# Narrower PE tiles for the state's read, float32r for its gates from part three, and one PE step for two products with the state

## The chip, the cores and the metric

The kernel runs on one core of a Trainium2 chip. Its time is the device time of one execution in microseconds; before the change the median of three runs is 759.64 us (759.14 to 759.84). The core has engines that run side by side and wait for each other through semaphores: TensorE (PE in the profile, with its weight loads as PEld) multiplies matrices from SBUF into PSUM, VectorE (DVE) and ScalarE (ACT) work element by element and move PSUM to SBUF, GpSimd (POOL) helps DVE with a few elementwise steps, and SyncE (SP) issues the DMAs. PSUM has 8 banks here, each 512 float32 columns wide (tile `PS`). A stationary operand that fills only a part of the 128x128 array leaves room for others beside it; `tile_position=(row, column)` says where it goes, and a piece of the array used so is called a tile of PE below.

## What is computed

Three layers follow each other. Attention with a small state (4 batches, 8 heads, 512 tokens, 32 state rows of 64 numbers a head), then a gated layer, then a softplus layer:

```python
scores = scale * np.matmul(x, state.transpose(0, 1, 3, 2))
...
xread = np.matmul(a, state)
scores2 = scale * np.matmul(state, x.transpose(0, 1, 3, 2))
...
sread = np.matmul(a2, x)
...
a = x @ w_a
b = x @ w_b
return (a * b @ w_out).astype(np.float32)
...
h = x @ w_in
g = np.maximum(h, 0.0) + np.log1p(np.exp(-np.abs(h)))
return (g @ w_out).astype(np.float32)
```

`a` and `a2` are softmaxes of the scores. A batch has 512 tokens from `xread` and 32 from `sread`, so there are 2176 tokens. The gated layer has 1536 hidden columns and the softplus layer 2048. All weights arrive in float64; the kernel reads their halves as integers and builds float32 from them.

## The kernel before

A planner at build time holds all the work as steps in program order. A step is one DVE or ACT instruction, or a group of matmuls on PE (class `Products`, closed by `end`, L493). The planner walks a clock with costs of its own; on each engine it takes, among the steps whose inputs it thinks ready, the one that stands first in program order and whose buffers it can place. An engine's queue is then fixed, and at run time each engine works through its queue in order. Nearly all instructions come from helpers: matmuls from L476, transposes from L491, copies and casts from L422 (ACT) or L423 (DVE), two-input DVE and POOL work from L430.

The gated layer runs in six parts of 256 hidden columns (`s` = 0 to 5; "part three" is `s` = 2), each over four batches `b`:

- `state_softmax(b)`, L726: transposes the scores with 8 PE transposes, makes the softmax over 32 state rows with six DVE instructions and an exponential on ACT, and transposes the result back with 8 more (`turned(e)`, L741). The last DVE instruction before these is the multiply with the reciprocal sum, L740.
- `state_w(s, bp, g)`, L765: the products of the state with the weights of part `s`, for two batches and four heads: 8 float32 matmuls with 64 rows and 32 columns each, in the eight 64x32 tiles of PE, into two banks. A cast and a subtract (`split_to`, L500) then make a high and a low float32r piece. A float32 matmul is two records in the profile, a float32r matmul one.
- `gates_of(s, b)`, L823, takes a batch's softmax times these products, 24 float32r matmuls of 512 columns (three for each float32 product, `three` at L479); `y_part`, L849, takes the gates times `w_out`, 24 more.
- `sread(b)`, L677, is the state's read of the tokens, in part 0 only: 16 float32 matmuls of 128 rows, 64 columns and 128 moving columns (two heads at once, L698), whose diagonal 64x64 blocks are what is wanted; then two scalings on ACT, two transposes and four copies into `srT`.
- `read_x(s)`, L792, gives the gates of the 128 state tokens: four float32 matmuls of 512 columns from `srt` and the weights `ab`, and `read_y` (L866) goes on with them. Parts 0 and 1 of it run in part 1, the others each in their own part.
- `bring`, `bring_wo`, `bring_w2` convert weights (L524: one ACT and five DVE or POOL instructions for 1024 columns).

The softplus layer (L979 on) follows with a loop over 4 quarters of the hidden columns, 4 batches and 4 steps.

Of the kernel before, what the change touches and what calls it, by code (L numbers as in the profile page):

```python
# [12 lines left out]
AF = mybir.ActivationFunctionType  # L13
# [4 lines left out]
P = 128  # L18
# [310 lines left out]
def attention_moe_moe2(ctx, tc, x, state, w_a, w_b, w_out, w_in, w_out2, out):  # L329
# [12 lines left out]
    B, H, S, D = x.shape  # L342
# [5 lines left out]
    KD = DM // P  # L348
# [4 lines left out]
    scale = 1.0 / float(D) ** 0.5  # L353
# [58 lines left out]
    def activation(o, i, func, **kw):  # L412
        also = [v for v in kw.values() if isinstance(v, Ref)]
        acc = [kw["accum_out"]] if "accum_out" in kw else []
        give = lambda: nc.scalar.activation(  # L415
            made(o), made(i), func, **{k: made(v) for k, v in kw.items()})
        plan.add({"act": (act_us(cols(o), in_psum(i)), give)}, [i, *also], [o, *acc])
# [82 lines left out]
    def split_to(i, hi, lo):  # L500
        copy(hi, i)
        tt(lo, i, hi.bitcast(F32), ALU.subtract)
# [102 lines left out]
    def xn(b, p, c):  # L605

        return xs[b][p].rearrange("q (h c d) -> q c h d", h=2, d=D)[:, c]
# [10 lines left out]
    for n, i in enumerate((zs, zt)):  # L618
        ps = Buf(K, 1)
# [14 lines left out]
    def quarter(b, i):  # L634

        return i ^ b % 2
# [40 lines left out]
    def sread(b):  # L677
        t = raw.pop(b)
        nm, sum2 = small(), small()
        nm_, sum_ = nm[0][:, 0:2], sum2[0][:, 0:2]  # L680
        reduce(nm_, t.all(), ALU.max)
        ts(nm_, nm_, -scale, ALU.mult)
        for g in range(2):
            activation(
                t[g], t[g], AF.Exp, bias=nm[0][:, g:g + 1], scale=scale,
                accum_out=sum2[0][:, g:g + 1],
            )
        ts(sum_, sum_, 1e-9, ALU.add)
        reciprocal(sum_)
        pa = turned(t)  # L690
        a2 = Buf(F, 2)
        copy(a2.all(), pa.all())
        pr = Buf(K, 2)
        m = Products()
        for g in range(2):
            for c in range(4):
                for j in range(2):
                    m.one(  # L698
                        pr[g][64 * j:64 * j + 64, 0:P].rearrange("p (h d) -> p h d", h=2),
                        a2[g][:, c * P + 64 * j:c * P + 64 * j + 64],  # L700
                        xn(b, 2 * g + j, c), c == 0, c == 3, us=0.23,
                    )
        m.end()

        for g in range(2):
            sd = a2[g][:, 0:P]
            activation(sd, pr[g][:, 0:P], AF.Identity, scale=sum2[0][:, g:g + 1])
            m = Products()
            m.turn(pr[g][:, P:2 * P], sd)
            m.end()  # L710
        for i in range(2):
            for g in range(2):
                src = pr[g][64 * i:64 * i + 64, P:2 * P]
                src = src.rearrange("p (j q n) -> p j q n", j=2, q=2)
                if b % 2:
                    src = src[:, :, ::-1]
                copy(
                    srT[64 * i:64 * i + 64, 2 * g:2 * g + 2, NS * b:NS * b + NS], src[:, :, i]
                )
# [42 lines left out]

        ab[s, p] = ab[s, p + 1] = fetch(("ab", s, p), 4)

    def state_w(s, bp, g):  # L765

        banks = Buf(K, 2)
        m = Products()
        for i in range(4):
            pp, half = divmod(i, 2)  # L770
            rows = slice(64 * half, 64 * half + 64)
            for j in range(2):
                b = 2 * bp + j
                q = quarter(b, i)
                m.one(
                    banks[j][32 * q:32 * q + 32], srow(sts[0], 2 * g + pp, half, NS * b, NS),
                    ab[s, 2 * g + pp][pp][rows, :], True, True, us=0.11,
                    tile_position=(64 * half, 32 * q),
                )
        m.end()  # L780
        if s == 0 and 2 * bp in G32:
            v = Buf(F, 2)
            copy(v.all(), banks.all())
            for j in range(2):
                sw[s, 2 * bp + j, g] = (v[j],)
            return
        h, l = Buf(R, 2, 8), Buf(R, 2, 6)
        split_to(banks.all(), h.all(), l.all())
        for j in range(2):
            sw[s, 2 * bp + j, g] = h[j], l[j]  # L790

    def read_x(s):  # L792

        ps = Buf(K, 1)
        m = Products()
        for p in range(KD):
            m.one(ps[0], srt[0][:, p * P:p * P + P], ab[s, p][p % 2], p == 0, p == KD - 1, us=0.87)
        m.end()
        t = Buf(F, 1)
        ab_ = t[0][:, 0:HW]  # L800
        copy(ab_, ps[0][:, 0:HW])
        tt(ab_, ab_, ps[0][:, HW:W], ALU.mult)
        pt = Buf(K, 1)
        m = Products()
        for j in range(2):
            m.turn(pt[0][:, j * P:j * P + P], t[0][:, j * P:j * P + P])
        m.end()
        if s == 0 and len(Y32) == B:
            gs[s] = Buf(F, 1)
            copy(gs[s][0][:, 0:HW], pt[0][:, 0:HW])  # L810
            return
        gs[s] = Buf(R, 1)
        split_to(pt[0][:, 0:HW], gs[s][0][:, 0:HW], gs[s][0][:, HW:W])

    gs, wo, y = {}, {}, {}

    def bring_wo(s):
        w = fetch(("wo", s), 2)
# [95 lines left out]
    scores_of(0)  # L914
    bring(0, 0)
    state_softmax(0)
    state_w(0, 0, 0)
    bring(0, 2)
    state_w(0, 0, 1)
    steps = [(s, b) for s in range(NHS) for b in range(B)]  # L920
    SREAD = 0
    pend = []
# [7 lines left out]
    for s, b in steps:  # L930
        if s == 0 and b == 0:
            scores_of(1)
        hl = gates_of(s, b)
        if s == 0:
            if b == 0:
                bring_wo(0)
                state_softmax(1)
                scores_of(2)
                state_w(0, 1, 0)
                state_w(0, 1, 1)  # L940
            if b == 1:
                state_softmax(2)
                scores_of(3)
            if b == 2:
                state_softmax(3)
        if s == SREAD:
            sread(b)
        if s and b == 0:
            if s > SREAD + 1:
                read_x(s)  # L950
            bring_wo(s)
        if s == SREAD + 1 and b < SREAD + 2:
            read_x(b)
        if s == SREAD + 1 and b == 3:
            for t in range(SREAD + 1):
                read_y(t)
        if s > SREAD and b == 2:
            read_y(s)
        if s + 1 < NHS:
            if b == 0:  # L960
                bring(s + 1, 0)
            if b == 1:
                bring(s + 1, 2)
                state_w(s + 1, 0, 0)
            if b == 2:
                state_w(s + 1, 0, 1)
                state_w(s + 1, 1, 0)
            if b == 3:
                state_w(s + 1, 1, 1)
        elif b:  # L970
            bring_w2(("in", 0) if b == 1 else ("out", 0) if b == 2 else ("in", 1))
        pend.append((s, b, hl))
        if len(pend) > 1:
            finish()
# [122 lines left out]
```

## Time and profile before

| | us |
|---|---|
| three runs, median | 759.64 |
| the profiled execution | 758.87 |
| its span, first to last instruction | 757.1 |
| PE busy / DVE busy / ACT busy in it | 733.0 / 583.4 / 401.8 |
| first matmul begins / last one ends | 7.78 / 749.97 |

The span is read from the left: until 7.78 us PE has no input; then the softmaxes and the first part set a time in which PE has waits; from 86 us on PE hardly stops until 749.97 us; a tail of 7.1 us brings the last results out. PE's granted clock is at its full level (2.4 GHz) except in the tail. Busy time counts records that overlap once.

### The profile page before, as it was taken

How to read it: one execution, taken by the hardware profiler on the slowest of the kernel's cores; microseconds unless marked ns; L12 is line 12 of the kernel's file. 1: busy time of each engine (PE TensorE's matmuls, PEld its weight loads, DVE VectorE, ACT ScalarE, POOL GpSimd, SP SyncE). 2: the span in 40 equal slices, each digit the busy share in tenths (PEclk: the TensorE clock that was granted, in tenths of full speed). 3: DMA queues.
4: the chain of work that ended last, by engine and by line, in shares of the span. 5: the costliest groups of instructions: out<-in, count | busy, mean ns of one | idle time of the engine just before them, and what ended most of it. 6: DMA issues, size and time to landing. Idle time of an engine off the chain costs nothing.

```text
span 757.1 us, 9417 instructions
## 1 busy us (share of the span) xinstructions
PE 733.0 (97%) x3828; PEld 581.8 (77%) x3828; DVE 583.4 (77%) x735; ACT 401.8 (53%) x644; POOL 32.7 (4%) x19
## 2 busy tenths in 40 slices
PE   5889999999999999999999999999999999999996
PEld 4447677777777777778888798888988889888895
DVE  4999987768677868889999767665769888665673
ACT  4767753232323424424395586656666667656562
POOL 0000000000001000000211100100110011100000
PEclk9999999999999999999999999999999999999999
DMA  9611321103112113133111000000111100001112
GB/s 309 205 59 54 130 93 54 58 1 112 56 44 68 56 56 111 56 110 114 56 56 56 1 1 1 0 1 1 55 57 56 55 1 1 1 0 56 56 56 70
DMA packets 22351, 45.17 MB, mean 60 GB/s; under 512 B 2212, under 2 KB 6308, under 8 KB 22308
## 3 DMA queue, kind: packets, MB, share of 16 engines
q1 hardware_dynamic: 21764, 43.52, 17.0%
q10 hardware_dynamic: 544, 1.05, 0.4%
q8 instruction: 30, 0.49, 0.3%
q14 instruction: 13, 0.11, 0.0%
HBM read 40.11 MB, written 4.46 MB: 59 GB/s over the span
## 4 chain that ended last, share of the span: by engine, by line
PE 77%; DVE 19%; issue 1%; DMA 1%; ACT 1%; SPq 0%; DVEq 0%
PE PS L476 76%; DVE SF L442 6%; DVE SF L430 5%; DVE SR L430 3%; DVE SM L448 2%; DVE SF L438 2%; PE PS L491 1%; DMA x<-in_x 1%; DVE xr L430 1%; ACT SF L415 0%; SPq L459 0%; DVE SM L453 0%; ACT SR L422 0%; DVE SR L423 0%; DVE xf L430 0%
## 5 line engine op out<-in xcount | busy, mean ns | idle before, releaser
L476 PE MATMUL PS<-SR 128*128 128x512 f32 (+2 forms) x1878 | 461.0, 378 | 2.5 <-DVE SF L430 1.2
L476 PEld LDWEIGHTS PS<-SR 128*128 128x128 f32 x1878 | 340.1, 188 | 71.2 <-issue 3.6
L415 ACT ACTIVATE SF<-SF 128x512 f32<-128x512 f32 (+3 forms) x259 | 165.7, 650 | 14.1 <-DMA SF<-in_moe_w_b 7.2
L476 PE MATMUL PS<-SR,xr 128*128 128x512 f32 (+2 forms) x568 | 159.3, 384 | 0.0
L430 DVE TENSOR_TENSOR SF<-SF,PS 128x1024 f32<-128x1024 f32 (+2 forms) x100 | 97.7, 985 | 47.9 <-PE PS L476 47.4
L422 ACT CAST SR<-SF 128x1024 fp32r<-128x1024 f32 (+3 forms) x103 | 75.5, 735 | 107.5 <-DVE SF L430 107.2
L442 DVE SCALAR_TENSOR_TENSOR SF<-SF 128x512 f32<-128x512 f32 (+4 forms) x139 | 131.6, 949 | 1.1
L476 PEld LDWEIGHTS PS<-SR,xr 128*128 128x128 f32 x568 | 105.0, 188 | 24.3 <-issue 2.6
L422 ACT COPY SF<-PS 128x1024 f32<-128x1024 f32 (+3 forms) x87 | 62.3, 737 | 110.2 <-PE PS L476 103.9
L476 PE MATMUL PS<-xr,SR 128*128 128x512 f32 x378 | 120.3, 392 | 0.0
L430 DVE TENSOR_TENSOR SR<-SF,SR 128x512 fp32r<-128x512 f32 (+3 forms) x96 | 82.9, 868 | 23.4 <-ACT SR L422 23.3
L442 DVE SCALAR_TENSOR_TENSOR SF<-PS,SF 128x512 f32<-128x512 f32 (+2 forms) x77 | 46.6, 605 | 54.9 <-ACT SF L415 54.9
L476 PEld LDWEIGHTS PS<-xr,SR 128*128 128x128 f32 x378 | 70.9, 188 | 16.8 <-DVE SF L430 0.8
L430 DVE TENSOR_TENSOR SF<-SF 128x512 f32<-128x512 f32 (+3 forms) x97 | 79.7, 822 | 1.7
L476 PE MATMUL PS<-SF 64*32 64x512 f32 (+2 forms) x592 | 65.2, 551 | 1.0 <-ACT SF L422 1.0
L438 DVE TENSOR_SCALAR SF<-SF 128x1024 uint32<-128x1024 uint32 x67 | 45.9, 689 | 18.8 <-ACT SF L415 18.4
L415 ACT ACTIVATE SF<-PS 128x512 f32<-128x512 f32 (+2 forms) x76 | 39.9, 526 | 30.8 <-PE PS L476 29.8
L430 POOL TENSOR_TENSOR SF<-SF 128x1024 f32<-128x1024 f32 x9 | 24.0, 2663 | 507.4 <-DVE SF L442 386.1
L476 PEld LDWEIGHTS PS<-SF 64*32 64x32 f32 (+1 forms) x592 | 22.0, 117 | 26.8 <-issue 22.6
L422 ACT CAST xr<-SF 128x1024 fp32r<-128x1024 f32 (+3 forms) x26 | 21.3, 821 | 33.9 <-DVE SF L430 33.9
L422 ACT CAST SR<-PS 128x1024 fp32r<-128x1024 f32 (+2 forms) x24 | 20.6, 866 | 20.1 <-PE PS L491 12.1
L476 PE MATMUL PS<-xr,xr 128*128 128x512 f32 x80 | 29.0, 391 | 0.0
(56 smaller groups left out, 274.1 us busy)
## 6 DMA issues: line engine op xcount, KB each, us to landing
SF<-in_moe_w_out SPq DMA_DIRECT2D x14, 1024.0 KB, 4.9
SF<-in_moe_w_in SPq DMA_DIRECT2D x8, 1024.0 KB, 5.4
SF<-in_moe_w_a SPq DMA_DIRECT2D x11, 512.0 KB, 4.1
SF<-in_moe_w_b SPq DMA_DIRECT2D x11, 512.0 KB, 5.0
x<-in_x SPq DMA_DIRECT2D x8, 512.0 KB, 9.9
out<-SF SPq DMA_DIRECT2D x13, 256.0 KB, 2.6
out<-xf SPq DMA_DIRECT2D x4, 256.0 KB, 2.6
SF<-in_moe_w_a ACTq DMA_DIRECT2D x1, 512.0 KB, 4.2
```

Of the source, the lines that this page charges most:

```text
L415: give = lambda: nc.scalar.activation(made(o), made(i), func, **{k: made(v) for k, v in kw.items()})
L422: "act": (act_us(n, ps), lambda: nc.scalar.copy(made(o), made(i))),
L430: put = lambda eng: lambda: eng.tensor_tensor(out=made(o), in0=made(a), in1=made(b), op=op)
L438: give = lambda: nc.vector.tensor_scalar(made(o), made(i), s1, None, op0=op0)
L442: give = lambda: nc.vector.scalar_tensor_tensor(out=made(o), in0=made(a), scalar=s, in1=made(b), op0=op0, op1=op1)
L448: give = lambda: nc.vector.tensor_reduce(out=made(o), in_=made(i), axis=AX.X, op=op)
L476: self.all.append(lambda: nc.tensor.matmul(made(o), made(w), made(x), start=first, stop=last, **kw))
L491: self.all.append(lambda: nc.tensor.transpose(made(o), made(i), ident))
```

## The change

`sread` takes one head a matmul: 32 matmuls a batch of 128 rows, 32 columns and 64 moving columns, head `i` at the columns `q` of PE in which its scores stand, four tiles side by side. What was a 128x128 result in one bank is 128x64, the scalings handle 64 columns, and the transposes give 64 rows instead of 128.

`state_w` is one step for both `g`: 16 matmuls into four banks, then two casts and two subtracts as before. At the start (`s` = 0, first two batches) it stays one `g` at a time. The two steps of parts 1 to 5 are put into the program at `b` = 2 and `b` = 3, where three places held four steps.

`read_x` splits `srt` once (512 columns) and the weights of a part (two splits of 1024 columns each) into float32r pieces from `s` = 2 on, and makes 12 float32r matmuls in place of four float32 ones. For `s` = 0 and 1 nothing changes in it.

```diff
-                for j in range(2):
+                for i in range(4):
+                    q = 32 * quarter(b, i)
                     m.one(
-                        pr[g][64 * j:64 * j + 64, 0:P].rearrange("p (h d) -> p h d", h=2),
-                        a2[g][:, c * P + 64 * j:c * P + 64 * j + 64],
-                        xn(b, 2 * g + j, c), c == 0, c == 3, us=0.23,
+                        pr[g][q:q + 32, 0:D], a2[g][:, c * P + q:c * P + q + 32],
+                        xn(b, 2 * g + i // 2, c)[:, i % 2], c == 0, c == 3, us=0.03,
+                        tile_position=(0, q),
                     )
...
-            sd = a2[g][:, 0:P]
-            activation(sd, pr[g][:, 0:P], AF.Identity, scale=sum2[0][:, g:g + 1])
+            sd = a2[g][:, 0:D]
+            activation(sd, pr[g][:, 0:D], AF.Identity, scale=sum2[0][:, g:g + 1])
             m = Products()
-            m.turn(pr[g][:, P:2 * P], sd)
+            m.turn(pr[g][0:D, P:2 * P], sd)
...
-    def state_w(s, bp, g):
-
-        banks = Buf(K, 2)
+    def state_w(s, bp, gs_=(0, 1)):
+
+        banks = {g: Buf(K, 2) for g in gs_}
         m = Products()
+        for g in gs_:
+            state_products(m, banks[g], s, bp, g)
+        m.end()
+        for g in gs_:
...
+            h, l = Buf(R, 2, 8), Buf(R, 2, 6)
+            split_to(banks[g].all(), h.all(), l.all())
...
+        whole = s < WHOLE
+        if not whole:
+            if not srparts:
+                srparts.append(split(srt))
+            whl = split(ab[s, 0], 6) + split(ab[s, 2], 6)
         m = Products()
         for p in range(KD):
-            m.one(ps[0], srt[0][:, p * P:p * P + P], ab[s, p][p % 2], p == 0, p == KD - 1, us=0.87)
+            c = slice(p * P, p * P + P)
+            w = [ab[s, p]] if whole else whl[p // 2 * 2:p // 2 * 2 + 2]
+            m.three(ps[0], [i[0][:, c] for i in ([srt] if whole else srparts[0])],
+                    [i[p % 2] for i in w], p == 0, p == KD - 1)
...
-                state_w(0, 1, 0)
-                state_w(0, 1, 1)
+                state_w(0, 1)
...
-                state_w(s + 1, 0, 0)
             if b == 2:
-                state_w(s + 1, 0, 1)
-                state_w(s + 1, 1, 0)
+                state_w(s + 1, 0)
             if b == 3:
-                state_w(s + 1, 1, 1)
+                state_w(s + 1, 1)
```

`state_products` holds the eight matmuls that stood in `state_w`, unchanged.

Since the planner orders all steps anew, queues change beyond the edited lines. DVE at the start, before the change; the third row is the cast of `state_w(0, 1, 0)`, the fourth its subtract, and then a weight conversion (`bring(0, 2)`) and the softmaxes' first reductions begin:

```order
L442 SCALAR_TENSOR_TENSOR SF<-SF 128x1024
L430 TENSOR_TENSOR SF<-SF 128x1024
L423 CAST SR<-PS 128x1024
L430 TENSOR_TENSOR SR<-PS,SR 128x1024
L438 TENSOR_SCALAR SF<-SF 128x1024
L448 TENSOR_REDUCE SM<-SF 128x2
L448 TENSOR_REDUCE SM<-PS 128x32
```

The same place of DVE's queue after the change:

```order
L442 SCALAR_TENSOR_TENSOR SF<-SF 128x1024
L430 TENSOR_TENSOR SF<-SF 128x1024
L438 TENSOR_SCALAR SF<-SF 128x1024
L448 TENSOR_REDUCE SM<-SF 128x2
L442 SCALAR_TENSOR_TENSOR SF<-SF 128x1024
L448 TENSOR_REDUCE SM<-PS 128x32
```

The cast has gone to ACT, the subtract stands some two dozen rows later beside that of the other `g`, and DVE's first work after its pause is now the conversion of `bring(0, 2)`. Up to the multiply of `state_softmax(2)` there are 52 DVE instructions both before and after the change; the sets differ by the cast, which left, and one subtract of `gates_of(0, 1)`, which came ahead of it.

PE in part 0, from the gates of batch 1 on, before the change. `x_82` marks `sread(0)`; the row of 32x512 is `state_w(1, 0, 0)`; the row with 6 is the first of four pieces of `y_part(0, 0)`; the last row begins with the 8 transposes of `turned(e)` of `state_softmax(2)`:

```order
L476 MATMUL PS<-x_82,SF 64x128 x16
L476 MATMUL PS<-SF 128x512 x2
L491 MATMUL PS<-ident,SF 128x128 x2
L476 MATMUL PS<-SF 32x256 x16
L476 MATMUL PS<-SF 32x512 x8
L476 MATMUL PS<-SR 128x512 x6
L491 MATMUL PS<-ident,SF 128x128 x16
```

And after the change:

```order
L476 MATMUL PS<-x_82,SF 32x64 x32
L476 MATMUL PS<-SF 128x512 x2
L491 MATMUL PS<-ident,SF 64x128 x2
L491 MATMUL PS<-ident,x_98 128x128 x8
L476 MATMUL PS<-SF 32x256 x8
L476 MATMUL PS<-SR 128x512 x6
L476 MATMUL PS<-SF 32x256 x8
L476 MATMUL PS<-SR 128x512 x12
L491 MATMUL PS<-ident,SF 128x128 x16
```

Three pieces of `y_part(0, 0)` now stand ahead of these transposes where one stood, `state_w(1, 0)` has moved behind them, and the second transposes of batch 3's tokens (`x_98`), which stood ahead of `sread(0)`, come here.

## Rows read from the trace of the kernel before

**Rows 1.** Busy time by stretch: stretch, length, then each engine's busy us (instructions).

```profile
20.00:86.00 66.00, 57.63 (x464) 36.82 (x465) 65.66 (x81) 47.49 (x72) 0.00 (x0) 1.00 0.30 101
86.00:330.00 244.00, 244.00 (x1257) 180.67 (x1257) 186.55 (x181) 89.21 (x104) 2.39 (x1) 1.00 0.20 68
330.00:400.00 70.00, 70.00 (x312) 57.76 (x311) 66.17 (x69) 38.02 (x53) 8.07 (x3) 1.00 0.25 83
400.00:750.00 350.00, 349.60 (x1672) 297.79 (x1670) 255.57 (x397) 216.66 (x404) 20.95 (x8) 1.00 0.07 25
```

**Rows 2.** Chain that ended last, to 110 us: start, us, what.

```profile
16.35 1.24 DVE SR L423
17.61 1.22 DVE SR L430
...
57.35 1.22 DVE SF L430
...
84.49 1.24 DVE SF L430
...
85.86 1.28 PE PS L491 x10
```

**Rows 3.** The same chain, its last piece.

```profile
747.29 3.41 DVE SF L430 x5
```

**Rows 4.** PE in order of time, to 100 us: start, us, what, count, idle before.

```profile
49.95 1.97 PE L476 MATMUL PS<-x,SF 128*64 128x128 f32 x32
51.84 1.98 PE L476 MATMUL PS<-SF 128*128 128x512 f32 x4
...
58.73 2.04 PE L491 MATMUL PS<-ident,SF 128*128 128x128 f32 x16
...
62.92 1.66 PE L476 MATMUL PS<-SR 128*128 128x512 f32 x6 [0.77 <-DVE SR L430]
...
85.86 1.28 PE L491 MATMUL PS<-ident,SF 128*128 128x128 f32 x10 [1.40 <-DVE SF L430]
```

**Rows 5.** PE in order of time, the read at 109 us.

```profile
109.21 3.60 PE L476 MATMUL PS<-SF 128*128 128x512 f32 x8
112.24 3.31 PE L476 MATMUL PS<-xr,SR 128*128 128x512 f32 x12
115.38 0.39 PE L491 MATMUL PS<-ident,SF 128*128 128x128 f32 x2
```

**Rows 6.** PE in order of time, its last matmuls.

```profile
744.37 2.20 PE L476 MATMUL PS<-SR 128*128 128x512 f32 x9
746.41 3.56 PE L476 MATMUL PS<-SR,xr 128*128 128x512 f32 x15
```

**Rows 7.** PE in order of time, products with the state, one group and two.

```profile
155.36 1.09 PE L476 MATMUL PS<-SF 64*32 64x512 f32 x16
...
156.72 0.39 PE L476 MATMUL PS<-SR,xr 128*128 128x512 f32 x1
...
195.59 1.95 PE L476 MATMUL PS<-SF 64*32 64x512 f32 x32
...
197.80 0.40 PE L476 MATMUL PS<-SR 128*128 128x512 f32 x1
```

**Rows 8.** PE from 13.36 to 13.42 us alone.

```profile
13.37 0.45 PE L476 MATMUL PS<-SF 64*32 64x256 f32 x8
```

**Rows 9.** ACT in order of time, the conversion that DVE's next one needs.

```profile
16.38 1.19 ACT L415 ACTIVATE SF<-SF 128x1024 f32<-128x1024 f32 x1
17.46 2.42 ACT L422 COPY SF<-PS 128x512 f32<-128x512 f32 x3
```

**Rows 10.** Groups by line and shape: count, busy us, mean ns, idle before.

```profile
L430 DVE TENSOR_TENSOR SR<-SF,SR 128x1024 fp32r<-128x1024 f32 x32 | 42.5, 1331 | 3.2 <-ACT SR L422 3.2
L422 ACT CAST SR<-SF 128x1024 fp32r<-128x1024 f32 x38 | 39.8, 1047 | 32.7 <-DVE SF L430 32.5
```

More of the change, by code (lines that the diff above doesn't have):

```diff
@@ L712, in sread @@
             for g in range(2):
-                src = pr[g][64 * i:64 * i + 64, P:2 * P]
-                src = src.rearrange("p (j q n) -> p j q n", j=2, q=2)
+                src = pr[g][0:D, P:2 * P].rearrange("p (j q n) -> p j q n", j=2, q=2)
                 if b % 2:
@@ L763, in bring, with state_products @@
         ab[s, p] = ab[s, p + 1] = fetch(("ab", s, p), 4)
-    def state_w(s, bp, g):
-        banks = Buf(K, 2)
+    def state_w(s, bp, gs_=(0, 1)):
+        banks = {g: Buf(K, 2) for g in gs_}
         m = Products()
+        for g in gs_:
+            state_products(m, banks[g], s, bp, g)
+        m.end()
+        for g in gs_:
+            if s == 0 and 2 * bp in G32:
+                v = Buf(F, 2)
+                copy(v.all(), banks[g].all())
+                for j in range(2):
+                    sw[s, 2 * bp + j, g] = (v[j],)
+                continue
+            h, l = Buf(R, 2, 8), Buf(R, 2, 6)
+            split_to(banks[g].all(), h.all(), l.all())
+            for j in range(2):
+                sw[s, 2 * bp + j, g] = h[j], l[j]
+    def state_products(m, banks, s, bp, g):
         for i in range(4):
@@ L779, in state_w @@
                 )
[L780 to L790, printed above, removed]
     def read_x(s):
         ps = Buf(K, 1)
+        whole = s < WHOLE
[3 more added lines that the diff above has]
+            whl = split(ab[s, 0], 6) + split(ab[s, 2], 6)
         m = Products()
         for p in range(KD):
-            m.one(ps[0], srt[0][:, p * P:p * P + P], ab[s, p][p % 2], p == 0, p == KD - 1, us=0.87)
+            c = slice(p * P, p * P + P)
+            w = [ab[s, p]] if whole else whl[p // 2 * 2:p // 2 * 2 + 2]
+            m.three(ps[0], [i[0][:, c] for i in ([srt] if whole else srparts[0])],
+                    [i[p % 2] for i in w], p == 0, p == KD - 1)
         m.end()
@@ L813, in read_x @@
         split_to(pt[0][:, 0:HW], gs[s][0][:, 0:HW], gs[s][0][:, HW:W])
-    gs, wo, y = {}, {}, {}
+    WHOLE = 2
+    gs, wo, y, srparts = {}, {}, {}, []
     def bring_wo(s):
@@ L916, in attention_moe_moe2 @@
     state_softmax(0)
-    state_w(0, 0, 0)
+    state_w(0, 0, (0,))
     bring(0, 2)
-    state_w(0, 0, 1)
+    state_w(0, 0, (1,))
     steps = [(s, b) for s in range(NHS) for b in range(B)]
```

## The prediction

> **What bounds the kernel now.** I read the busy time by stretches first. From 86 us to 750 us PE is busy all the time but 0.4 us [rows 1]; from 20 to 86 us DVE is (65.66 of 66) and PE is not (57.63). So there are two regimes, and each part of the change is worth what its regime gives. The chain of waits says the same: from 16.35 us it runs along DVE almost without a break and goes over to PE at 85.86 us [rows 2], stays there until the last matmul ends at 746.41 + 3.56 = 749.97 us [rows 6], and ends with five DVE additions of 3.41 us [rows 3] and a store. A microsecond of PE work taken out behind 86 us is a microsecond of the span, as long as DVE keeps up; one taken out ahead counts only if DVE delivers earlier too. PE's timeline shows where it waits in the first regime: before 58.73 us often, behind it 0.77 us at 62.92 and 1.40 us at 85.86 [rows 4].
>
> **read_x of parts three to six.** It removes four float32 matmuls in each of four parts and adds twelve of float32r. What one read takes: it begins at 109.21 us, twelve float32r matmuls follow, and the next record begins at 115.38 [rows 5], 6.17 us for both. Float32r matmuls of 512 columns take 0.227 us each in a row (nine from 744.37 to 746.41 us [rows 6]), twelve 2.72. The float32 read is 6.17 - 2.72 = 3.45 us, the new one 2.72, so 0.73 us less each and 2.9 us for four. All four lie behind 86 us. Against that stand 8 splits of 1024 columns and one of 512: a subtract is 1.33 us and a cast 1.05 [rows 10], half of that for 512 columns, in sum 8.5 x 1.33 = 11.3 us of DVE and 9 of ACT. I cost them at nothing: between 86 and 330 us DVE is idle for 244 - 186.55 = 57 us and ACT for 155 [rows 1], and in the new order all splits but the last one or two stand far ahead of their read. From 330 to 400 us DVE has only 3.8 us left [rows 1]; a split that falls there could push others. Bounds for the whole edit: 3.5 us gained, 8.4 us lost if the 11.3 us meet no idle time and 2.9 us stay as the gain.
>
> **state_w in one step.** No matmul goes. Between records before and after, eight products alone (16 records) take 156.72 - 155.36, less the 0.227 of the record behind that stands between, 1.13 us; two groups that happen to be adjacent (32 records) take 197.80 - 195.59 - 0.23 = 1.98 us [rows 7]. Joining saves 2 x 1.13 - 1.98 = 0.28 us of filling and emptying the array. Four groups a part were one adjacent pair and two alone and become two pairs, so it is once a part, five times, and once more for batches 2 and 3 of part 0: 6 x 0.28 = 1.7 us, 0.28 of it ahead of 58.73 us. Four banks are held at once; the adjacent pair at 195.59 us held four too, and PE has no wait there [rows 1, 7]. Bounds: 1.7 us gained, 10 us lost (a rival below).
>
> **sread.** Today a read is 51.84 - 49.95 = 1.89 us for 32 records [rows 4]. The new one has 64 records of 64 columns in four tiles. No row shows that form. The nearest one is the group in eight tiles: its second half adds 1.98 - 1.13 = 0.85 us for 16 records, two a tile, so a record of 512 columns holds its tile for 427 ns, 0.83 ns a column, while the tiles run side by side [rows 7]. By that, 64 columns hold a tile for 53 ns, 16 records a tile make 0.85 us, and with the 0.28 us of filling it is 1.1 us: 0.8 us less a read, 3.2 us for four, of which the first 0.8 lies ahead of 58.73 us. Lower end: 0.85 us a read. Upper end: no overlap at all, 64 x 53 + 280 ns = 3.7 us, 1.8 us more than today. I take 1.1, because the eight matmuls that begin before 13.42 us had all been started within 60 ns of 13.37 [rows 8], so starting records in different tiles is not what limits them. What is new is the short moving part.
> Here a rule speaks against the edit. The Trainium skill, "TensorEngine Tiling (Array Packing)", section "Instruction Overhead", says that a matmul has about 60 cycles of overhead, that a free dimension of 1 takes as long as one of 60, and that tiling should not be taken from a dimension that is already small; 64 is nearly there. If that overhead (about 25 ns by the page "TensorE: Matmul & The Clock Gate", section "Back-to-back issue gap") were paid by each of 64 records one after another, a read would be an estimated 1.9 us, and the edit would give nothing. Eight matmuls of different tiles within 60 ns [rows 8] speak against paying it in a row.
> The scalings get half as wide and the transposes half as tall; ACT and DVE do as many instructions as before, and I count no gain.
>
> **The sum.** PE has 2.9 + 1.7 + 3.2 = 7.8 us less to do. How much of it shows depends on when DVE lets PE go. I take the multiply of state_softmax(2), since PE's transposes wait for it: it runs from 57.35 for 1.22 us [rows 2], and PE begins at 58.73 [rows 4]. Ahead of it stand 52 DVE instructions in both orders. The cast that opened the busy time at 16.35 us (1.26 us to the next [rows 2]) is gone, a subtract of 1.13 us (a 1.22 us instruction, overlapped) has come, and the first piece is now a conversion that needs ACT's, done when ACT goes on at 17.46 us [rows 9]. So the multiply ends 17.46 - 16.35 - 1.26 + 1.13 = 1.0 us later, and PE begins at 59.7 us.
> Before, 749.97 - 58.73 = 691.24 us followed. Now 7.8 - 0.8 - 0.28 = 6.7 us are gone of it; two more pieces of y_part(0, 0), six matmuls each, 2.7 us together, have been done by then; state_w(1, 0, 0), 1.1 us, has moved behind. That leaves 691.24 - 6.7 - 2.7 + 1.1 = 682.9 us, with the two waits of 0.77 and 1.40 us still in it. PE would end at 742.6 instead of 749.97, 7.4 us earlier. The pieces of y_part are filler: work that PE does in the time in which it waited.
> Does a later point of DVE bind more? At the multiply of state_softmax(3), which ends at 85.7 us [rows 2], DVE's new order has 70 instructions ahead instead of 86: conversions for later parts and the state subtracts of part 1, about 12.6 us at today's durations, stand behind it now. It would come 11 us earlier, while PE is only 7 to 9 us earlier there, so the 1.40 us may go too; I leave that as the good end. The tail of 7.1 us stays: the last steps are unchanged.
> Against the profiled execution: its span is 757.1 us, 758.87 with what lies around it; less 7.4 that is 751.5. The median of the three runs is 0.8 us above that execution, so I predict 752.2 us.
>
> **The rivals.**
> The narrow tile gives nothing: the read's time goes by records, not by columns, and stays at 1.9 us or grows. For it: 32 records take 1.89 us now, 59 ns each, and the number doubles. Against it: the state's products take less than that per record in eight tiles. With 1.9 us the three reads behind 58.73 us give back 2.4 us: 754.6. With no overlap, 3.7 us, they give back 7.8: 760.0.
> DVE binds the first part longer: the queues were all rewritten, and a few waits of 0.7 to 1.4 us more on PE as those of today [rows 4] cost about 3 us: 755.2. For it: DVE has no idle time there; against it: the counts above.
> Banks, the slower side: a joined step needs four of eight banks, and PE's queue runs in order, so while it waits for a bank everything behind it waits, the gates and y_part of other batches too. If each of the ten joined steps of parts 1 to 5 waited for one pass that empties two banks (1.22 us for a DVE instruction of 1024 columns, as at 17.61 us [rows 2]), that is 12.2 us: 764.4, slower. It outweighs the gain from 0.74 us a step. Against it: four banks were held at the adjacent pairs without a wait.
> Splits on the path: the casts and subtracts for read_x come when DVE is full and PE waits for gates or for converted weights. If the 11.3 us all land there, 763.5. Against it: 57 us of idle time, read_x has other PE work around it, and the splits stand early. That the change doesn't do what it says, with the splits' time on the path and no gain at all, lies inside this one.
>
> **How the numbers follow.** The forecast, with 0 to 3 us more or less of waiting, 749 to 755 us: 0.66. The narrow tile at no gain: 0.12, of which a fourth near 760. DVE in the first part: 0.10. Banks: 0.06. Splits: 0.06. A measurement of this kernel can tell a change from none at about 0.2%, 1.5 us, so faster means below 758.1 us. The forecast, the DVE case and most of the tile's case are faster: 0.66 + 0.10 + 0.09 = 0.85, with 0.01 more from splits that land only in part. Between 758.1 and 761.2 lie a few mixtures: 0.06. Slower: banks 0.04, splits 0.03, tile 0.01, together 0.08. The range runs from 748.7 (the 2.2 us of waits gone and the read at 0.85 us) to 757.8, which takes in the tile without gain and the DVE case.
>
> **What would show it.** In the profile after: the reads in part 0 take 1.1 us each; each read_x from part three on is twelve float32r matmuls with no wait ahead; records of 64x512 stand in 32s; PE is busy without a break from some 78 us; its transposes for state_softmax(2) begin near 60 us; the last matmul ends near 742.6 us, and the tail keeps its 7.1 us. POOL may take a few conversions or splits more. I am wrong if PE shows waits of a microsecond at the joined steps or at the gates between 86 and 400 us, if a read takes 1.9 us, or if the multiply of state_softmax(2) ends past 62 us.

## The result, and the profile after

The changed kernel takes 751.34 us, the median of four runs (750.74 to 752.21); the kernel before takes 759.65 us beside it (759.14 to 759.84). The ratio is 0.9891, with a 95% interval of 0.9879 to 0.9903. The execution that was profiled is the slowest of the four, 752.21 us. Its page, span and first part:

```profile
span 750.4 us, 9721 instructions
...
PE 725.7 (97%) x3972; PEld 582.0 (78%) x3972; DVE 590.7 (79%) x740; ACT 407.2 (54%) x650; POOL 50.2 (7%) x26
```

PE is 7.3 us less busy than before (733.0) and the span is 6.7 us shorter (757.1). The same stretches as in [rows 1], in the same columns:

```profile
20.00:86.00 66.00, 61.00 (x608) 39.20 (x606) 64.42 (x79) 51.00 (x80) 0.00 (x0) 1.00 0.26 89
86.00:330.00 244.00, 242.32 (x1329) 185.51 (x1328) 202.76 (x193) 94.08 (x108) 20.39 (x8) 1.00 0.24 78
330.00:400.00 70.00, 69.70 (x310) 57.39 (x309) 66.19 (x74) 40.38 (x57) 5.16 (x2) 1.00 0.22 76
```

Two things differ from what [rows 1] showed. In the first stretch PE does 3.4 us more (57.63 before), so its waits there are fewer. In the second, where it had no idle time, it now has 1.68 us, and POOL works 20.39 us there instead of 2.39.

The chain of waits up to 95 us (start, us, what), which went along DVE until 85.86 us before [rows 2], now leaves DVE at 34.68 us and stays on PE from 49.77 us until 163 us, shortly before the first of the two waits below; its last piece is still five DVE additions [rows 3], from the end of PE's work:

```profile
33.41 1.23 DVE SF L430
34.68 3.71 PE PS L476 x8
38.41 1.02 ACT SF L422
39.48 3.70 PE PS L476 x8
...
45.40 1.99 ACT SR L422 x2
...
49.77 0.66 PE PS L491 x4
50.42 4.66 PE PS L476 x72
...
61.90 1.75 PE PS L491 x16
...
94.67 15.51 PE PS L476 x61
...
740.21 3.41 DVE SF L430 x5
```

PE in order of time, the rows that answer to [rows 4, 6, 7]:

```profile
8.84 1.09 PE L491 MATMUL PS<-ident,SF 128*128 128x128 f32 x4 [8.84 <-DMA SF<-in_state]
...
52.07 1.10 PE L476 MATMUL PS<-x,SF 128*32 128x64 f32 x64
53.10 1.98 PE L476 MATMUL PS<-SF 128*128 128x512 f32 x4
...
58.88 3.02 PE L476 MATMUL PS<-SR 128*128 128x512 f32 x12
61.74 1.91 PE L491 MATMUL PS<-ident,SF 128*128 128x128 f32 x16
...
72.80 1.95 PE L476 MATMUL PS<-SF 64*32 64x512 f32 x32
74.67 1.09 PE L491 MATMUL PS<-ident,SF 128*128 128x128 f32 x8
...
742.50 0.39 PE L476 MATMUL PS<-xr,SR 128*128 128x512 f32 x1
```

A read of the state takes 53.10 - 52.07 = 1.03 us instead of 1.89 [rows 4]. No idle time stands ahead of the transposes at 61.74 us, of the joined step at 72.80, or of anything between 49.77 and 169 us. PE's last matmul ends at 742.50 + 0.39 = 742.89 us instead of 749.97 [rows 6].

The new waits stand in the second stretch. Three engines in order of time at 165 us and at 270 us:

```profile
165.53 2.39 POOL L430 TENSOR_TENSOR SR<-SF,SR 128x1024 fp32r<-128x1024 f32 x1 [2.32 <-ACT SR L422]
165.59 3.41 DVE L430 TENSOR_TENSOR SR<-SF,SR 128x1024 fp32r<-128x1024 f32 x1
168.92 1.54 DVE L430 TENSOR_TENSOR SF<-SF,PS 128x256 f32<-128x256 f32 x2
169.38 0.44 PE L491 MATMUL PS<-ident,SF 128*128 128x128 f32 x2 [0.51 <-DVE SF L430]
...
269.53 2.74 POOL L430 TENSOR_TENSOR SR<-SF,xr 128x1024 fp32r<-128x1024 f32 x1 [52.46 <-PE PS L476]
269.94 3.41 DVE L430 TENSOR_TENSOR SR<-SF,xr 128x1024 fp32r<-128x1024 f32 x1
274.87 0.44 PE L491 MATMUL PS<-ident,SF 128*128 128x128 f32 x2 [1.17 <-DVE SF L430]
```

Each time a subtract of `read_x`'s splits went to POOL, and the subtract on DVE beside it took 3.41 us, where [rows 10] has 1.33 on the mean. Behind it in DVE's queue stands the 256-column multiply of the state tokens' gates (at 270 us with one other subtract between), and PE's transposes wait for that: 0.51 + 1.17 = 1.68 us, all that PE lacks in this stretch.

### The profile page after: what moved, and what is told of

Same layout as the page of the kernel before. It is cut to its first block, busy times and chain, and to the rows that moved or that the text cites. A ratio compares the mean times of both kernels' runs of the same rounds, so it can differ in the third digit from the quotient of the medians.

```text
span 750.4 us, 9721 instructions
## 1 busy us (share of the span) xinstructions
PE 725.7 (97%) x3972; PEld 582.0 (78%) x3972; DVE 590.7 (79%) x740; ACT 407.2 (54%) x650; POOL 50.2 (7%) x26
## 4 chain that ended last, share of the span: by engine, by line
PE 84%; DVE 10%; ACT 2%; DMA 1%; issue 1%; SPq 0%; DVEq 0%
PE PS L476 82%; DVE SF L442 4%; DVE SF L430 2%; DVE SR L430 2%; PE PS L491 2%; ACT SF L415 1%; DMA x<-in_x 1%; DVE SF L438 1%; ACT SF L422 1%; DVE SM L448 1%; ACT SR L422 1%; SPq L459 0%; DVE xf L442 0%; ACT xf L415 0%; DVE xf L430 0%
## 5 line engine op out<-in xcount | busy, mean ns | idle before, releaser
L476 PE MATMUL PS<-SR 128*128 128x512 f32 (+2 forms) x1904 | 492.9, 377 | 0.1
L430 DVE TENSOR_TENSOR SF<-SF,PS 128x1024 f32<-128x1024 f32 (+2 forms) x126 | 116.8, 942 | 34.4 <-PE PS L476 33.8
L476 PE MATMUL PS<-xr,SR 128*128 128x512 f32 x424 | 142.7, 390 | 0.8 <-DVE SR L430 0.8
L442 DVE SCALAR_TENSOR_TENSOR SF<-SF 128x1024 uint32<-128x1024 uint32 (+4 forms) x120 | 108.1, 905 | 0.6
L430 DVE TENSOR_TENSOR SR<-SF,SR 128x1024 fp32r<-128x1024 f32 (+3 forms) x78 | 74.3, 955 | 18.0 <-ACT SR L422 17.7
L442 DVE SCALAR_TENSOR_TENSOR SF<-PS,SF 128x512 f32<-128x512 f32 (+1 forms) x74 | 45.2, 610 | 53.6 <-ACT SF L415 53.5
L430 DVE TENSOR_TENSOR SF<-SF 128x512 f32<-128x512 f32 (+2 forms) x88 | 70.4, 800 | 1.4
L476 PE MATMUL PS<-SF 64*32 64x512 f32 (+2 forms) x560 | 51.0, 554 | 3.0 <-ACT SF L422 2.4
L491 PE MATMUL PS<-ident,SF 128*128 128x128 f32 (+1 forms) x128 | 19.6, 285 | 13.3 <-DMA SF<-in_state 8.8
L491 PEld LDWEIGHTS PS<-ident,SF 128*128 128x128 f32 (+1 forms) x128 | 15.2, 144 | 20.1 <-issue 10.7
```

Source lines behind the costliest of these rows:

```text
L430: put = lambda eng: lambda: eng.tensor_tensor(out=made(o), in0=made(a), in1=made(b), op=op)
L442: give = lambda: nc.vector.scalar_tensor_tensor(out=made(o), in0=made(a), scalar=s, in1=made(b), op0=op0, op1=op1)
L476: self.all.append(lambda: nc.tensor.matmul(made(o), made(w), made(x), start=first, stop=last, **kw))
L491: self.all.append(lambda: nc.tensor.transpose(made(o), made(i), ident))
```

## The experiments

Each was timed beside the kernel before, which took between 759.46 and 759.55 us on the median. Ratios are to that, with the 95% interval.

### Each part alone

**read_only**: `sread` as in the change, all else as before.

```diff
-                for j in range(2):
+                for i in range(4):
+                    q = 32 * quarter(b, i)
...
+                        xn(b, 2 * g + i // 2, c)[:, i % 2], c == 0, c == 3, us=0.03,
+                        tile_position=(0, q),
```

> The kernel before with the narrow tiles of sread alone. Theory 1 (each microsecond of PE work counts behind the point at which DVE lets PE go): four reads give 3.4 us of PE work back, of which the one behind 86 us (0.85 us) surely shows and the three ahead of it only as far as DVE's queue allows: 757 to 759 us against 759.65. Theory 2 (the new order of the queues makes the gain, since a shorter read moves the planner): below 756.5 us. If the tile gave nothing: 759 to 760 us.

Measured: 751.90 us, ratio 0.9901 [0.9886, 0.9916]. The read alone gives 7.65 us, nearly as much as the whole change, and over twice the 3.4 us of PE work that it takes away (4 x 0.86). That is where the second theory had it.

**readx_only**: float32r reads from part three on (`WHOLE = 2`), all else as before.

```diff
+            whl = split(ab[s, 0], 6) + split(ab[s, 2], 6)
...
-            m.one(ps[0], srt[0][:, p * P:p * P + P], ab[s, p][p % 2], p == 0, p == KD - 1, us=0.87)
+            m.three(ps[0], [i[0][:, c] for i in ([srt] if whole else srparts[0])],
```

> The kernel before with float32r in read_x from part three on, alone; no split of read_x is on POOL in this order. Theory 1: four reads of 0.73 us less behind 86 us, 2.9 us: 756.7 us, PE without waits of over 0.3 us between 86 and 400 us. Theory 2 (the splits come back as waits): 758.5 us or more, with a wait ahead of a read_x or its transposes.

Measured: 756.95 us, ratio 0.9969 [0.9958, 0.9981], 2.6 us less, near the first theory. Between 86 and 400 us PE has the wait of before, 1.40 us at 87.05, and one of 0.44 us at 157.09.

**statew_only**: the joined `state_w`, all else as before.

```diff
-                state_w(s + 1, 0, 1)
-                state_w(s + 1, 1, 0)
+                state_w(s + 1, 0)
```

> The kernel before with the joined state products alone. Theory 1 (only the filling and emptying of the array counts): 6 x 0.28 = 1.7 us, 758.0 us. Theory 2 (what matters is that the cast of state_w(0, 1, 0) leaves DVE and the subtracts of part 1 stand later, so that DVE lets PE go earlier): 756 us or less, with the waits of 0.77 and 1.40 us in part 0 gone. Rival (four banks held): 761 us or more, with waits at the joined steps.

Measured: 760.93 us (759.36 to 762.03), ratio 1.0017 [1.0008, 1.0025]: no gain, rather a loss. Of its eleven executions three took 759.36 to 759.54 us, as long as the kernel before, at a mean granted clock of 0.997; the other eight took 760.70 us and more, at 0.995 to 0.997, the profiled one 761.79 us at 0.995. Its timeline of PE at 88 us:

```profile
88.19 2.67 PE L491 MATMUL PS<-ident,SF 128*128 128x128 f32 x16 [1.90 <-DVE SF L430]
90.52 9.62 PE L476 MATMUL PS<-SR 128*128 128x512 f32 x36
```

Its stretches there (columns as in [rows 1], the granted clock third from the end):

```profile
90.00:92.00 2.00, 2.00 (x9) 1.71 (x8) 1.97 (x3) 2.00 (x3) 0.00 (x0) 0.50 0.35 137
92.00:94.00 2.00, 2.00 (x8) 1.64 (x7) 1.93 (x3) 0.26 (x1) 0.00 (x0) 0.74 0.00 0
94.00:98.00 4.00, 4.00 (x20) 3.29 (x19) 2.60 (x3) 1.57 (x2) 0.00 (x0) 1.00 0.31 76
```

The wait that stood at 85.86 us before, 1.40 us [rows 4], is 1.90 us here. Behind it the granted clock falls to 0.50, the lower of its two levels (1.2 GHz), from 90 to 92 us, and the 36 matmuls from 90.52 us on take 9.62 us, where 36 x 0.227 = 8.2 would do [rows 6]. The last matmuls of `y_part(0, 3)`, found in both traces by their place in the queue, end at 121.44 us, against 118.34 before. Of these 3.1 us 0.68 is the later arrival of the state (PE's first matmul begins at 8.46 instead of 7.78 us) and 1.4 the clock; the longer wait and the other order make the rest. Then the kernel catches up: at the end of `y_part(1, 3)`, (2, 3), (3, 3) and (4, 3) it is 2.72, 2.31, 1.89 and 1.47 us behind, 0.42 us less each part. PE does not wait at the joined steps, so the rival of the banks is not what costs.

Another loss lies in the softplus layer. At 385 us PE is 1.5 us behind the kernel before, at 403 us 2.8, and 2.9 at the end. In between it waits 0.98 us at 400.99, for a DVE subtract that stands behind an instruction stretched beside POOL:

```profile
397.04 2.75 POOL L430 TENSOR_TENSOR SF<-SF 128x1024 f32<-128x1024 f32 x1 [7.23 <-DVE SF L442]
398.03 2.30 DVE L442 SCALAR_TENSOR_TENSOR SF<-SF 128x512 f32<-128x512 f32 x1
...
400.99 2.35 PE L476 MATMUL PS<-SR 128*128 128x512 f32 x9 [0.98 <-DVE SR L430]
```

### Work against order

The read's cost in the planner fell with its matmuls, from 16 x 0.23 to 32 x 0.03 us, and with it all queues changed. Two kernels take the one without the other.

**read_old_order** has the narrow read, with the planner's costs of the wide one. All engines' queues are those of before, but for the read itself.

```diff
-                        xn(b, 2 * g + i // 2, c)[:, i % 2], c == 0, c == 3, us=0.03,
+                        xn(b, 2 * g + i // 2, c)[:, i % 2], c == 0, c == 3, us=0.115,
...
-            activation(sd, pr[g][:, 0:D], AF.Identity, scale=sum2[0][:, g:g + 1])
+            activation(sd, pr[g][:, 0:D], AF.Identity, as_cols=P, scale=sum2[0][:, g:g + 1])
```

> The narrow read alone, with its planner costs set to the sums of the wide one, so that every engine's queue stands in the order of the kernel before; only the work of the four reads is less (3.4 us). Theory 1 (the read's work makes the gain of 7.65 us seen with the read alone): 756 us or less. Theory 2 (the order makes it; ahead of 86 us DVE sets the time and only the last of the four reads counts): 758.7 us, with the waits of 1.18, 0.77 and 1.40 us in part 0 grown.

Measured: 759.35 us (758.72 to 761.22), ratio 1.0001 [0.9993, 1.001].

**order_only** is the kernel before with one number changed, so that the planner gives every queue the order of read_only; the read stays wide.

```diff
-                        xn(b, 2 * g + j, c), c == 0, c == 3, us=0.23,
+                        xn(b, 2 * g + j, c), c == 0, c == 3, us=0.06,
```

> The kernel before, with the planner told 0.06 us for each matmul of the wide read, so that every engine's queue stands in the order of the kernel with the narrow read alone; the work is that of before. Theory 1 (work): 759.5 us. Theory 2 (order): the three waits in part 0 shrink by about 3.6 us, and PE has its old 3.4 us of work to do: 755 to 756 us.

Measured: 755.35 us, ratio 0.9946 [0.9934, 0.9959].

| | wide read | narrow read |
|---|---|---|
| queues of before | 759.5 | 759.35 |
| queues of read_only | 755.35 | 751.90 |

With the queues of before the narrow read is worth 0.15 us, which the interval does not tell from nothing, with the new ones 3.45; the new queues alone are worth 4.15. Where the work goes in the first case stands in PE's timeline of read_old_order:

```profile
57.44 1.67 PE L476 MATMUL PS<-SR 128*128 128x512 f32 x6 [1.38 <-DVE SF L430]
...
63.25 1.66 PE L476 MATMUL PS<-SR 128*128 128x512 f32 x6 [0.87 <-DVE SR L430]
...
68.37 0.50 PE L491 MATMUL PS<-ident,SF 128*64 128x128 f32 x2 [0.84 <-ACT SF L415]
...
86.19 1.28 PE L491 MATMUL PS<-ident,SF 128*128 128x128 f32 x10 [2.26 <-DVE SF L430]
```

The transposes at 86.19 us come when DVE lets them, as at 85.86 before [rows 4], and the wait ahead of them has grown from 1.40 to 2.26 us. The idle times that the timeline prints behind PE's first matmul add to 9.1 us before, 11.7 in read_old_order, 5.3 in order_only and 5.5 in read_only. In the stretch from 20 to 86 us PE is busy 55.06 us in the first of these experiments and 61.00 in the second:

```profile
20.00:86.00 66.00, 55.06 (x558) 34.08 (x558) 65.65 (x80) 47.07 (x73) 0.00 (x0) 1.00 0.30 102
```

```profile
20.00:86.00 66.00, 61.00 (x500) 40.10 (x485) 64.27 (x77) 50.32 (x78) 0.00 (x0) 1.00 0.25 87
```

The order thus decides whether PE has filler where it would wait, and by that whether work taken from it counts.

### The splits on POOL

**no_pool_split**: the change, with the subtracts of `read_x`'s splits kept on DVE.

```diff
-        if not ps:
+        if not ps and pool:
...
-            whl = split(ab[s, 0], 6) + split(ab[s, 2], 6)
+            whl = split(ab[s, 0], 6, False) + split(ab[s, 2], 6, False)
```

> The changed kernel with the subtracts of read_x's splits barred from POOL; the two that POOL takes (at 165.5 and 269.5 us) go to DVE. Theory 1 (while POOL subtracts, DVE's own subtract takes 3.41 us instead of 1.22 and PE waits 0.51 and 1.17 us for what is queued behind it): 1.7 us less, 749.6 us against 751.3, no wait of PE between 100 and 400 us. Theory 2 (DVE is simply late there; with one more subtract it is as late): 751.3 us, waits as before.

Measured: 749.18 us, ratio 0.9864 [0.9851, 0.9878], 2.2 us below the change. From 86 to 330 us PE has no idle time any more, though POOL works there as long as in the change (20.06 and 20.39 us) and DVE too (202.44 and 202.76):

```profile
86.00:330.00 244.00, 244.00 (x1338) 187.44 (x1337) 202.44 (x193) 95.05 (x110) 20.06 (x8) 1.00 0.24 78
```

The queues of PE and ACT hold the same instructions in the same order as in the change, and in DVE's and POOL's only the two subtracts have changed places with two additions of weight conversions. At the same places of PE's queue the change is 0.87 us behind no_pool_split at 154 us, 1.58 at 187 and 2.99 from 297 us on: it loses 0.71 and 1.41 us at the two waits, somewhat more than PE's idle time there, and nothing elsewhere behind 54 us. So what counts is not how much POOL does, but which DVE instruction stands beside it. The planner has this cost in its clock, but too small: `cost += 0.7 * max(0.0, min(pool_end - now, cost))` adds at most 0.7 of DVE's own 1.22 us, 0.85 us, where the two subtracts took 2.19 us longer (3.41 instead of 1.22).

**pool_none**: the change with all two-input work barred from POOL.

```diff
-        if not ps:
+        if not ps and not POOL_OUT:
```

> The changed kernel with all two-input work barred from POOL, in every layer. Theory 1 (while POOL works, DVE's instruction beside it is stretched by about as much as POOL takes off it, so POOL's help is worth nothing and only its bad moments cost): about 749.2 us as with the two splits alone barred, no wait of PE of over 0.3 us behind 86 us. Theory 2 (POOL's help is needed where DVE is full, from 330 us on and in the softplus layer): 751 us or more, with waits of PE on DVE between 330 and 450 us.

Measured: 747.43 us (746.93 to 748.00), ratio 0.9841 [0.9827, 0.9854], 3.9 us below the change and 1.8 us below what the first theory gave. The stretch behind 400 us, in no_pool_split and then here:

```profile
400.00:735.00 335.00, 334.50 (x1607) 285.70 (x1606) 244.74 (x383) 210.97 (x393) 23.34 (x9) 1.00 0.07 23
```

```profile
86.00:400.00 314.00, 314.00 (x1649) 245.34 (x1648) 271.38 (x278) 136.71 (x168) 0.00 (x0) 1.00 0.22 74
400.00:735.00 335.00, 335.00 (x1613) 286.80 (x1612) 240.01 (x391) 212.19 (x394) 0.00 (x0) 1.00 0.08 26
```

In 335 us PE gets through 6 matmuls more, with no idle time in it, and DVE, which does eight instructions more, is busy 4.7 us less. Compared at the same places of PE's queue, the whole gain over no_pool_split lies at three waits of PE that are gone here, near 391, 408 and 564 us (0.56, 0.75 and 0.4 us).

**before_pool_none**: the same bar in the kernel before.

```diff
-        if not ps:
+        if not ps and not POOL_OUT:
```

> The kernel before with all two-input work barred from POOL. Theory 1 (most of what POOL costs lies in the softplus layer, as short waits of PE, and was there before the change): 759.5 - 1.7 = 757.8 us. Theory 2 (the cost came with the change, whose splits made DVE's time scarce): 759.5 us.

Measured: 758.23 us, ratio 0.9983 [0.9974, 0.9992], 1.2 us less. Of the 3.9 us that the bar gives to the change 2.2 are the splits; the other 1.7 are near what it gives in the kernel before, where the gain lies at two such waits, near 423 and 575 us.

### The joined steps, on top of the rest

**no_join**: no_pool_split with the four single `state_w` steps of before.

```diff
-                state_w(s + 1, 0)
+                state_w(s + 1, 0, 1)
+                state_w(s + 1, 1, 0)
```

> Narrow read and float32r in read_x with its subtracts barred from POOL, but the state products in four steps a part as before. Theory 1 (joining is worth 0.28 us a part, as records show): 749.18 + 1.4 = 750.6 us. Theory 2 (joining gave nothing alone, 759.5 us in its undisturbed executions, since the banks' emptying or the order takes it back): 749.3 us or less.

Measured: 750.20 us, ratio 0.9877 [0.9861, 0.9892]; joining is worth 1.0 us here (749.18 us in no_pool_split; the intervals of the two ratios overlap, the times, 749.96 us and more against 749.35 and less, do not). PE in no_join has a wait behind a single step:

```profile
201.28 1.09 PE L476 MATMUL PS<-SF 64*32 64x512 f32 x16
203.54 0.74 PE L476 MATMUL PS<-SR,xr 128*128 128x512 f32 x2 [1.17 <-DVE SF L430]
```

**pool_none_nojoin**: the same with POOL barred altogether.

```diff
-                state_w(s + 1, 0)
+                state_w(s + 1, 0, 1)
+                state_w(s + 1, 1, 0)
```

> Narrow read and float32r in read_x with POOL barred, and the state products in four steps a part. Theory 1 (joining is worth what its records save, 0.28 us a part, 1.4 us): 747.43 + 1.4 = 748.8 us, PE without new waits behind 86 us. Theory 2 (joining is worth its waits for banks, which DVE free of POOL does away with): 747.4 us.

Measured: 748.35 us, ratio 0.9853 [0.984, 0.9867]; joining is worth 0.9 us (again the intervals overlap and the times do not). What a part takes stands in PE's timeline, as the distance from one part's last `state_w` step to the next one's. Single steps:

```profile
201.24 1.09 PE L477 MATMUL PS<-SF 64*32 64x512 f32 x16
...
253.71 1.09 PE L477 MATMUL PS<-SF 64*32 64x512 f32 x16
```

The same in pool_none, with the joined ones:

```profile
200.54 1.95 PE L477 MATMUL PS<-SF 64*32 64x512 f32 x32
...
252.59 1.95 PE L477 MATMUL PS<-SF 64*32 64x512 f32 x32
```

That is 52.47 and 52.05 us, 0.42 less a part, as in statew_only. Not all of it arrives: at the end of `y_part(1, 3)` pool_none is 0.56 us behind pool_none_nojoin, and at the end of `y_part(4, 3)` 0.70 ahead, which it keeps to the end.

### Float32r for the first two reads too

**whole_none**: no_pool_split with `WHOLE = 0`, so that all six parts of `read_x` are float32r.

```diff
-    WHOLE = 2
+    WHOLE = 0
```

> The changed kernel with subtracts barred from POOL and float32r in read_x from part one on. Theory 1: two more reads of 0.73 us less, 749.18 - 1.5 = 747.7 us. Theory 2 (the splits for parts one and two fall where DVE is full and PE has just caught up): 749 us or more, with waits of PE between 86 and 150 us.

Measured: 751.08 us, ratio 0.9889 [0.9875, 0.9902], 1.9 us above no_pool_split, on the side of the second theory. At 117 us an instruction of a weight conversion on POOL again stretches its neighbour on DVE:

```profile
117.10 2.79 POOL L430 TENSOR_TENSOR SF<-SF 128x1024 f32<-128x1024 f32 x1 [6.56 <-DVE SF L442]
117.66 3.31 DVE L442 SCALAR_TENSOR_TENSOR SF<-SF 128x1024 uint32<-128x1024 uint32 x1
```

PE waits 1.78 us for DVE ahead of 125.49 us, and 0.88 us ahead of 95.95, where no_pool_split has no wait. An earlier wait, 1.90 us ahead of 27.38, behind which the granted clock is 0.50 from 28 to 30 us, is made up for: the first read of the state begins at 51.20 us, in no_pool_split at 51.19.

**pool_none_whole**: the same with POOL barred.

```diff
-    WHOLE = 2
+    WHOLE = 0
```

> The same, and float32r in read_x from part one on. Theory 1 (the loss of float32r from part one on, 751.08 against 749.18 us, came from DVE instructions stretched beside POOL, 3.31 us at 117.7 us ahead of a wait of 1.78): 1.5 us less than with POOL out alone, about 747.7 us. Theory 2 (the earlier splits crowd DVE in part 0 and 1 by themselves): 750 us or more.

Measured: 747.14 us (746.89 to 747.53), ratio 0.9838 [0.9825, 0.9852]. The time is near the first theory's, but the gain over pool_none is 0.3 us instead of its 1.5, with intervals that overlap. What the two reads save on PE (1.5 us) comes back in part as waits of 0.88 and 0.55 us near 95 and 110 us. pool_none and pool_none_whole are the fastest that were run, and both beat the change by some 4 us.

## Why the prediction was right, and where not

The time (752.2 forecast, 751.34 measured) and the end of PE's work (742.6 and 742.89) came out, but several terms were wrong and cancelled, so that the number is in part luck.

| step | forecast, us | measured, us |
|---|---|---|
| one read of the state | 1.1 | 1.03 |
| the narrow read in the kernel | 3.2 | 0.15 with the old queues, 3.45 with the new |
| new queues of the read's change | a wait or two, kept out of the sum | 4.15 |
| `read_x` | 2.9 | 2.6 alone |
| `state_w` joined | 1.7 | loss of 1.4 alone, gain of 0.9 to 1.0 on top of the rest |
| splits | 0 | 2.2 lost through POOL |

Along one row of kernels the steps add up: the read with its new queues 7.65 us (759.55 to 751.90), float32r in `read_x` without POOL 1.7 (to 750.20), joining 1.0 (to 749.18), and 2.2 lost through POOL (to 751.34). That is 8.2 us, where 8.3 was measured and 7.4 forecast. The lower end of the range does not come out of its terms: 752.2 less 2.2 us of waits and 0.25 us for each of three reads is 749.3, not 748.7; nothing else rests on it.

**The read.** The tile of 64 columns is as short as the forecast had it from [rows 7]: 64 records in 1.03 us, 16 ns each. The rival "the narrow tile gives nothing" falls. The rule of the Trainium skill, "TensorEngine Tiling (Array Packing)", section "Instruction Overhead", that tiling should not be taken from a dimension that is already small, does not hold here: if each record paid the 25 ns of "TensorE: Matmul & The Clock Gate", section "Back-to-back issue gap", one after another, the read would be an estimated 1.6 us and more. Across four tiles that is not paid in a row.

**Work for time.** The step that failed is "PE has 7.8 us less to do", less what lies ahead of 58.73 us, with the waits kept in. It treated PE behind 58.73 us as bound by its own work, though [rows 4] showed that the transposes at 85.86 us came when DVE let them. Up to there, work taken from PE becomes wait unless the queues change; read_old_order shows it. The new queues were seen (two more pieces of `y_part(0, 0)` ahead of the transposes), yet their gain was booked as a mere shift of work. They give more than the work does: the waits of 0.77 and 1.40 us that the sum kept "still in it" are gone, which the forecast had only as the good end.

**When DVE lets PE go.** The multiply of `state_softmax(2)` was to end at 59.6 us, and PE to begin at 59.7. It ended at 61.5 us (60.27 + 1.23), within the bound of 62. Of the 1.9 us, 1.06 is the state's later arrival: PE's first matmul begins at 8.84 instead of 7.78 us. But the transposes did not wait for it. The multiply of `state_softmax(3)` ended at 76.25 us instead of 85.73, 9.5 us earlier where 11 was forecast, and the wait of 1.40 us went. Behind 61.74 us came 681.15 us, where the forecast had 682.9. The rival "DVE binds the first part longer" falls.

**read_x.** A float32r read takes 2.72 us, from the start of its first record to the start of the next work, as the forecast had it, and without a wait a part takes 53.20 us with the float32 read (read_only, from 219.77 to 272.97) and 52.47 with the other (pool_none_nojoin, above), 0.73 us less, as forecast; readx_only gives 2.6 of the 2.9 us. The splits had been given no cost because of DVE's idle time, and the rival had priced them as 11.3 us of DVE work. Neither was it: the cost was that two of them went to POOL. "POOL may take a few conversions or splits more" stood in the forecast with no price. The two waits ahead of `read_x`'s transposes are 1.68 us, and without them the time is 2.2 us less. One of the forecast's own signs of being wrong, a wait of a microsecond at the gates between 86 and 400 us, thus came: 1.17 us at 274.87. The form of the rival holds, its size does not.

**state_w.** Each joined part saves 0.42 us, where the forecast had 0.28; five parts are 2.1 us instead of 1.4. The step that failed is that this goes straight into the time. Alone, the edit gives it away at two places. In part 0, where DVE still releases PE, the queues come in another order, the wait at 88.19 us is longer, and in the profiled execution the clock falls; in the softplus layer 1.3 us more go at the wait at 401 us, behind POOL. On top of the other parts the first two parts take back about half, and 0.9 to 1.0 us are left. That the order of part 0 is the cause, and not the joined step in it, is argued from the place of the waits; no run has single steps in the joined order, and none joined steps alone with POOL barred. The rival of the banks falls: no idle time stands ahead of any joined step.

**The tail** nearly kept its length: 750.4 - 742.89 = 7.5 us against 7.1.

## What to carry to other kernels

In a stretch where another engine releases the bottleneck, price the work removed and the new order apart: keep the planner's old cost for the new work, and give the old work the new cost, and two runs tell them apart. A cost that a planner holds for a step is itself a knob, worth 4.15 us here without any change of the work. Before work is handed to a helper engine, look in the trace at what its neighbour's instructions take beside it.

## What the runs showed of the hardware

**POOL and DVE exclude each other.** A DVE instruction with two inputs from SBUF that starts while POOL works on two SBUF tiles does all its work after POOL's end. At 165.53 + 2.39 = 167.92 us POOL ends, and DVE ends at 169.00; at 269.53 + 2.74 = 272.27, DVE at 273.35; both 1.08 us later, whatever the overlap. In all the traces together 44 DVE instructions of this kind with 1024 columns start so, and every one ends 1.08 or 1.09 us after POOL. The same 1.08 us follow two other POOL instructions at 119.56 and 214.66 us, and with 512 columns it is 0.55 us, as here:

```profile
462.79 2.50 POOL L430 TENSOR_TENSOR SR<-SF,SR 128x1024 fp32r<-128x1024 f32 x1 [52.39 <-ACT SR L422]
463.07 2.77 DVE L430 TENSOR_TENSOR SF<-SF 128x512 f32<-128x512 f32 x1
```

An instruction that has one input in PSUM is not held up; beside POOL's 160.81 to 163.20 us this one takes its usual 1.22 us:

```profile
160.81 2.39 POOL L430 TENSOR_TENSOR SF<-SF 128x1024 f32<-128x1024 f32 x1 [38.87 <-DVE SF L442]
...
162.19 1.22 DVE L430 TENSOR_TENSOR SF<-SF,PS 128x1024 f32<-128x1024 f32 x1 [1.51 <-PE PS L476]
```

The Trainium skill says this in "SBUF — State Buffer", section "SBUF: two separate sides": GpSimd and a DVE instruction with two SBUF inputs share a pair of ports, whoever starts first holds it for the whole instruction, and the other is blocked fully. The traces agree, to 0.01 us. The other way round POOL waits: begun at 320.28 us, behind a DVE instruction of 320.06, one took 3.28 us instead of 2.4. With 2.4 us on POOL against 1.22 on DVE, POOL's help is worth nothing where such an instruction stands next in DVE's queue.

**Clock.** The granted clock fell to 0.50 behind statew_only's wait of 1.90 us at 88.19 and behind whole_none's 1.90 us at 27.38. Behind the changed kernel's 1.17 us at 274.87 it stayed at 1.00, and also behind read_old_order's 2.26 us at 86.19. The length of the last wait alone does not tell which it will be.
